# Sketched attention and a two-layer MLP on one core: token order 4gg+g, every x block turned by TensorE, shared PSUM banks, new orders

## The chip, the cores and the metric

The kernel runs on one core of one Trainium2 chip. The core has five engines that run side by side, each with its own queue of instructions in a fixed order: TensorE (PE, matrix products; PEld is its weight load), VectorE (DVE), ScalarE (ACT), GpSimd (POOL) and SyncE (SP, which here only issues transfers). Sixteen DMA engines move data between the chip's memory (DRAM) and the on-chip SBUF. Matrix products land in PSUM, which has eight banks of 128 partitions by 512 fp32 values.

The metric is the device time of one execution in microseconds (us), lower is better. A profile is one such execution recorded by the hardware; its span runs from the first to the last instruction.

## The reference

Attention with a polynomial sketch, then a layer norm with an MLP on the concatenated heads. B = 4 batches, H = 4 heads, S = 1088 tokens, D = 32, r = 8; q, k and v are float32. S1, S2 and the two MLP weights come as float64.

```python
def phi(x):                                  # 64 features a token and head
    a = np.einsum('rd,bhsd->bhsr', S1, x)
    b = np.einsum('rd,bhsd->bhsr', S2, x)
    return np.einsum('bhsi,bhsj->bhsij', a, b).reshape(*x.shape[:-1], r * r)
q_p, k_p = phi(q), phi(k)
kv  = np.einsum('bhsf,bhsd->bhfd', k_p, v)
z   = np.sum(k_p, axis=2)
num = np.einsum('bhsf,bhfd->bhsd', q_p, kv)
den = np.einsum('bhsf,bhf->bhs', q_p, z)[..., None] + 1e-06
x   = (num / den).transpose(0, 2, 1, 3).reshape(B, S, 128)
xn  = (x - mean(x)) / sqrt(var(x) + 1e-06) * g_ln
out = x + np.maximum(xn @ w_ch1, 0.0) @ w_ch2    # 128 -> 512 -> 128
```

## The kernel before

**Tiles.** The 1088 tokens of a batch are 32 runs of 34: run gg has 32 tokens, numbered 8g+u (g = 0 to 3, u = 0 to 7), and two rest tokens. Token 8g+u of run gg sits on partition 32g+gg of tile u, so a batch is 8 tiles of 128 tokens and a ninth (u = 8) of 64 rest tokens. Behind the attention four tiles make a chunk: chunks 2b and 2b+1 belong to batch b (c = 0 to 7), chunks 8 and 9 hold the rest tokens of batches 0, 1 and of 2, 3.

**Loads.** `ld` and `ld_u` (L115, L125) bring q and k with head and run on the partitions; `ld_v` (L133) brings v of one head, with 4 outer steps (g) of 32 runs in DRAM; `ld_vr` (L141) brings the rest tokens of v; `ld_w` (L150, L152) the MLP weights, 512 KB each. All but the two `ld_s` (S1, S2 on ACT's queue) and `ld_g` (g_ln, on POOL's) go through SP's queue. The framework gives SP's transfers eight semaphores in turn, so that each waits until the eighth before it has landed.

**A batch, in steps.**

- `turn_g`, `turn_u`, `turn_r` (L404, L412, L421; DVE): transposes of 32 by 32 blocks put q and k, head by dimension on the partitions and token on the free axis, into qT and kT. There is one pair for even and one for odd batches.
- `k_feat` (L451; PE) and `k_tok` (L460; DVE): a and b of k, turned to tokens on the partitions (kf). Batch 0 goes another way (`k_dir`, `k_cp`, `k_prod0`). `k_prod` (L85; POOL): the 64 products a token and head (kp). `k_sum`, `k_zs`, `k_sc`, `k_sccp` (L475, L483, L489, L497): the denominator's row for q.
- `k_val` (L504; PE): kv in bank KV; `k_vcp` (ACT), `k_spr` (L519; PE), `k_rcp` (ACT): kv copied and transposed into kvr.
- `q_feat` (L572; PE), `q_tok` (L581; DVE, two halves), `q_ac`, `q_den`, `q_rec` (DVE: product, sum and reciprocal for the denominator, units 0 to 4 and 4 to 9), `q_a2` and `q_prod` (L85; POOL: tiles a and qp), `q_turn` (L619; DVE: qp transposed into qpT). Batch 0 has `q_dir`, `q_ac0`, `q_b0`, `q_prod0` on PE and DVE.
- `num` (L633; PE): the numerator into banks X and Y, `num_cp` and `num_r` (ACT): copied into xT (features on the partitions).

**A chunk, in steps.** `hid` (L734; PE, one 128x512 product for each of four groups of hidden units, into bank M, N or O) and `relu` (L742; ACT) read xT. `sec` (L750; PE, four products a tile into one bank) reads hT. `fin` (L763; DVE) is sec times 1/sigma plus x, into ob; `store` (L784) sends ob out by SP, again with 4 outer steps of 32 runs, and `store_r` (L793) the rest tokens of a batch, one by SP and one by ACT. The layer norm's gain and mean are folded into w1 (`c_cg`, `fold`), so only 1/sigma is left: `st_bn`, `st_ag` (DVE), `st_pow` (L723; POOL).

**Rows of x.** `st_bn` and `fin` need x with tokens on the partitions. For chunks 0, 1, 8 and 9, `row_pe` (L684) transposes xT on PE into bank KV and `row_cp` copies it with ACT. For chunks 2 to 7 it goes through DRAM: `row_turn` (L693; DVE, blocks of 32 into xh), `row_wr` (L697; one transfer by SP into xd), `row_rd` (L702; four transfers back into x, each with 4 outer steps of 32). Two buffers of hT and ob, four of xT and x are reused in turn; ob takes the chunks in the order 0, 1, 2, 3, 8, 4, 5, 6, 7, 9.

**What sets the order.** Each step is an `op`, and a string `PROGRAM` lists them; an engine's queue holds its steps in the order of that string. `fill n w` puts n products of ones, w columns wide, on PE; nothing reads them. The weights' steps `w_ex` to `w_add` turn float64 words into float32 (s: S1, S2; 1 and 2: the MLP weights).

```python
through_dram = set((2, 3, 4, 5, 6, 7, ))     # L671
order = [0, 1, 2, 3, 8, 4, 5, 6, 7, 9]       # ob and hT: even place buffer 0, odd place buffer 1
```

Of the kernel before, what the change touches and what calls it, by code (L numbers as in the profile page):

```python
# [25 lines left out]
def kernel(  # L26
# [374 lines left out]
    @op  # L401
    def turn_g(x, b, g0, g1):
        dst, src = turned[x]
        dve.transpose(  # L404
            _ap(dst[b % 2], 0, P, 32 * g0, [[32, g1 - g0], [P, 8], [1, 32]]),
            src[b][:, 256 * g0 : 256 * g1],
        )
# [383 lines left out]
    def store_r(eng, c, i):  # L791
        b = 2 * (c - 8) + i
        by[eng].dma_start(  # L793
            out=bass.AP(out.tensor, out.offset + (b * S + 32) * DM,
                        [[DM, 2], [G * DM, 32], [1, DM]]),
            in_=obs[turn_of(c)][64 * i : 64 * i + 64, 0:P],
# [18 lines left out]
    q_dir 0 4 N; w_e3 V 1 0 256; ld_vr S 1 0; w_add G 1 256 512; turn_r q 0; turn_u q 0 4 8;
    k_val 0; w_e3 V 1 256 512; q_cp A 0 4 N 16 24; q_ac0 0 4 N 0; w_add G 1 0 256; q_den 0 0 4;
    q_rec 0 0 4; ld_vr S 1 1; w_low A 2 0 512; q_dir 4 9 O; w_mul G 1 0 256; q_b0 0 4 N 0;
    k_vcp A 0; q_prod0 0 2 N 0; w_mul G 1 256 512; q_prod0 2 4 N 0; k_spr 0; q_cp A 4 9 O 16 24;
    q_turn 0 2; k_rcp A 0; fold N 0 256; ld S k 2 0 34; turn_g k 1 0 4; num 0 0 2;
    fold_cp A N 0 256; turn_r k 1; num_cp A 0 0 0 2; q_turn 2 4; num_cp A 0 1 0 2; hid M 0 0 0 2;  # L820
    q_ac0 4 9 O 4; q_den 0 4 9; ld S q 2 0 34; hid N 0 1 0 2; q_rec 0 4 9; relu A M 0 0 0 2;
    turn_r q 1; ld_v S 2 0; num 0 2 4; q_b0 4 9 O 4; relu A N 0 1 0 2; q_prod0 4 9 O 4;
    ld_v S 2 1; fold M 256 512; ld_v S 2 2; num_cp A 0 1 2 4; num_cp A 0 0 2 4; ld_v S 2 3;
    row_pe 0 K; fold_cp A M 256 512; q_turn 4 9; ld_vr S 2 0; row_cp A 0 K; hid N 0 2 0 2;
    ld_vr S 2 1; hid M 0 3 0 2; relu A N 0 2 0 2; w_bits V 2 0 512; relu A M 0 3 0 2; num 0 4 9;
    turn_g q 1 0 4; w_mant A 2 0 512; ld S k 3 0 34; w_add G 2 0 512; hid M 0 1 2 4; turn_r k 2;
    num_r A 0; turn_g k 2 0 4; num_cp A 0 0 4 8; num_cp A 0 1 4 8; k_feat 1; relu A M 0 1 2 4;
    w_ex V 2 0 512; row_pe 1 K; ld S q 3 0 34; k_tok 1; w_exf A 2 0 512; hid M 0 3 2 4;
    ld_v S 3 0; turn_r q 2; row_cp A 1 K; k_prod G 1 5 9; w_e2 V 2 0 512; hid N 0 0 2 4;
    ld_v S 3 1; relu A M 0 3 2 4; st_bn 1; k_sum 1; relu A N 0 0 2 4; ld_v S 3 2; hid M 1 1 0 4;  # L830
    k_zs 1; turn_g q 2 0 4; ld_v S 3 3; ld_vr S 3 0; k_prod G 1 0 5; k_sc 1; ld_vr S 3 1;
    hid N 0 2 2 4; relu A M 1 1 0 4; k_sccp V 1; st_bn 0; q_feat 1; relu A N 0 2 2 4; st_ag 0;
    hid N 1 0 0 4; w_e3 V 2 0 512; k_val 1; st_pow 0; turn_r k 3; relu A N 1 0 0 4; q_tok 1 0;
    turn_g k 3 0 4; w_mul G 2 0 512; hid N 1 2 0 4; k_vcp A 1; turn_r q 3; q_tok 1 1; sec O 0 3;
    relu A N 1 2 0 4; q_ac V 1 0 4; q_den 1 0 4; sec O 0 2; q_ac V 1 4 9; q_rec 1 0 4; st_ag 1;
    q_a2 G 1 0 4; turn_g q 3 0 4; sec O 0 1; q_prod G 1 0 4; sec O 0 0; q_den 1 4 9; q_rec 1 4 9;
    hid M 1 3 0 4; fin O 0 0; fin O 0 1; q_a2 G 1 4 9; fin O 0 3; fin O 0 2; k_feat 2; q_turn 0 4;
    q_prod G 1 4 9; relu A M 1 3 0 4; store S 0; sec O 1 0; k_tok 2; sec O 1 1; k_prod G 2 5 9;
    q_turn 4 9; k_spr 1; sec O 1 2; k_rcp A 1; k_sum 2; num 1 0 9; k_prod G 2 0 5; k_zs 2; k_sc 2;
    num_cp A 1 1 4 8; sec O 1 3; num_cp A 1 1 0 4; k_sccp V 2; num_cp A 1 0 0 4; st_pow 1;  # L840
    num_r A 1; num_cp A 1 0 4 8; row_turn 2; k_val 2; row_turn 3; row_wr S 2; fin O 1 0;
    row_wr S 3; fin O 1 3; q_feat 2; fin O 1 2; k_vcp A 2; fin O 1 1; store S 1; hid N 2 0 0 4;
    q_tok 2 0; q_tok 2 1; row_rd S 2 3; hid M 2 1 0 4; relu A N 2 0 0 4; row_rd S 2 0;
    q_ac V 2 0 4; row_rd S 2 2; hid N 2 2 0 4; q_den 2 0 4; relu A M 2 1 0 4; q_rec 2 0 4;
# [69 lines left out]
```

## Time and profile before

| what | us |
|---|---|
| median of 3 runs (139.23 to 141.09) | 140.34 |
| the profiled execution | 141.0 |
| its span | 139.2 |
| mean TensorE clock granted, share of full | 0.891 |

How the views are read. The table of engines gives busy time and its share of the span. In the row of 40 slices each digit is the busy share of 3.48 us in tenths; PEclk is the clock that TensorE was granted. In the list of waits a row names who waited for whom, the total in us, how often, and the longest. In a table of windows the columns are from:to, length, busy us (and instructions) of PE, PEld, DVE, ACT and POOL, the clock granted, the mean busy share of the 16 DMA engines and GB/s. In a timeline the columns are start, duration, engine, line, operation, output<-input with shapes, and how many instructions the row merges; in brackets the idle time ahead of it and who ended it. A PE product of fp32 shows as two records, so x10 is five products. The chain of waits follows the work that ended last backwards. The lines themselves stand in the prediction.

### The profile page before, as it was taken

What the parts mean: (1) busy time and instruction counts of PE and PEld (TensorE: products, weight loads), DVE (VectorE), ACT (ScalarE), POOL (GpSimd) and SP (SyncE); (2) the same over time, 40 slices, a digit from 0 to 9 for tenths busy, and PEclk for the clock granted to TensorE, in tenths of its full rate; (3) what the DMA queues carried; (4) which work ended last, traced back from release to release, by engine and by line L of the source; (5) the groups of instructions that cost most, each with busy time, mean ns of one, the idle gap of its engine ahead of it and who ended that gap; (6) DMA issues with size and microseconds to landing.
All of it is one profiled execution on the core that took longest, in us unless ns stands there. A gap on an engine that the chain in (4) does not pass through costs nothing.

```text
span 139.2 us, 3266 instructions
## 1 busy us (share of the span) xinstructions
PE 105.5 (76%) x1336; PEld 72.0 (52%) x1336; DVE 75.8 (54%) x225; ACT 39.6 (28%) x99; POOL 49.4 (36%) x62
## 2 busy tenths in 40 slices
PE   5998598999986899999105999907999999970000
...
PEclk9999855699999999999975799996899999999555
...
GB/s 137 238 132 227 315 111 245 158 101 235 177 99 68 16 64 151 57 79 77 24 0 56 19 153 66 78 87 26 0 0 37 196 30 66 82 49 0 36 102 31
DMA packets 14023, 13.32 MB, mean 96 GB/s; under 512 B 1848, under 2 KB 11832, under 8 KB 14008
## 3 DMA queue, kind: packets, MB, share of 16 engines
...
q8 instruction: 10, 0.16, 0.5%
q10 hardware_dynamic: 164, 0.07, 0.2%
q14 instruction: 5, 0.04, 0.1%
q0 software_dynamic: 32, 0.00, 0.0%
...
## 4 chain that ended last, share of the span: by engine, by line
DMA 46%; SPq 16%; DVE 14%; PE 10%; POOL 4%; issue 3%; ACT 3%; DVEq 0%; ACTq 0%
DMA vn<-in_v_dram 15%; DMA x<-xd 12%; DMA xd<-xh 9%; SPq L702 9%; DMA kn<-in_k_dram 5%; DMA out_dram<-ob 4%; PE X L633 4%; SPq L133 3%; POOL qp L85 3%; DVE st L710 3%; PE M L734 3%; DVE qpT L619 3%; PE PO L750 3%; ACT xT L80 2%; DVE xh L693 2%
## 5 line engine op out<-in xcount | busy, mean ns | idle before, releaser
L734 PE MATMUL M<-xT,w 128*128 128x512 f32 (+1 forms) x72 | 34.8, 604 | 5.0 <-ACT hT L742 4.6
L742 ACT ACTIVATE hT<-M 128x512 f32<-128x512 f32 (+2 forms) x44 | 21.4, 500 | 36.5 <-PE M L734 30.1
L750 PEld LDWEIGHTS PO<-w,hT 128*128 128x128 f32 x208 | 25.1, 194 | 7.0 <-DVE ob L763 3.2
L750 PE MATMUL PO<-w,hT 128*128 128x128 f32 x208 | 26.4, 279 | 1.9 <-DVE ob L763 1.4
L723 POOL TENSOR_TENSOR rstd<-va,mhalf 128x4 f32<-128x4 f32 (+1 forms) x10 | 9.6, 957 | 48.7 <-DVE va L717 48.5
L710 DVE BATCH_NORM_STATS2 st<-x 128x6 f32<-128x128 f32 x32 | 7.0, 280 | 27.1 <-DMA x<-xd 27.0
L734 PEld LDWEIGHTS M<-xT,w 128*128 128x128 f32 x72 | 12.3, 201 | 15.2 <-ACT hT L742 10.3
L85 POOL TENSOR_TENSOR kp<-kf 128x1024 f32<-128x1024 f32 (+3 forms) x8 | 15.2, 1916 | 3.6 <-ACT kf L80 2.2
L85 POOL TENSOR_TENSOR qp<-a,fq 128x1024 f32<-128x1024 f32 (+1 forms) x6 | 13.0, 2171 | 0.4
L619 DVE STREAM_TRANSPOSE qpT<-qp 128x1280 f32<-128x1280 f32 (+2 forms) x9 | 11.1, 1228 | 2.5 <-POOL qp L85 2.4
L80 ACT COPY xT<-X 128x256 f32<-128x256 f32 (+1 forms) x18 | 5.4, 361 | 17.3 <-PE X L633 17.3
L633 PE MATMUL X<-qpT,kvr 32*32 32x288 f32 (+2 forms) x384 | 9.4, 404 | 0.3 <-DVE qpT L619 0.3
L750 PEld LDWEIGHTS X<-w,hT 128*128 128x128 f32 x64 | 7.8, 192 | 1.4 <-issue 1.4
L237 PE MATMUL M<-ones 128*128 128x256 f32 (+2 forms) x16 | 7.2, 574 | 1.5 <-DVE ones L181 1.5
L750 PE MATMUL X<-w,hT 128*128 128x128 f32 x64 | 8.0, 275 | 0.0
L475 PE MATMUL KV<-kf 128*32 128x32 f32 x72 | 1.7, 212 | 8.0 <-DVE kf L460 8.0
L763 DVE SCALAR_TENSOR_TENSOR ob<-PO,rstd,x 128x128 f32<-128x128 f32 x24 | 6.7, 337 | 1.8 <-PE PO L750 1.8
L633 PEld LDWEIGHTS X<-qpT,kvr 32*32 32x32 f32 x384 | 5.2, 119 | 3.6 <-issue 2.1
L305 POOL TENSOR_TENSOR mant<-mant,low 128x256 f32<-128x256 f32 (+1 forms) x3 | 2.9, 988 | 11.5 <-ACT mant L283 11.5
L581 DVE STREAM_TRANSPOSE fq<-X 128x576 f32<-128x576 f32 x6 | 4.4, 754 | 4.1 <-PE X L572 4.1
L504 PE MATMUL KV<-kp,vn 128*32 128x64 f32 x288 | 5.1, 221 | 1.2 <-DMA vn<-in_v_dram 1.1
L475 PEld LDWEIGHTS KV<-kf 128*32 128x32 f32 x72 | 1.2, 121 | 9.1 <-DVE kf L460 8.2
(115 smaller groups left out, 123.7 us busy)
## 6 DMA issues: line engine op xcount, KB each, us to landing
...
```

The source lines that it names most:

```text
L80: act.copy(o, i)
L85: by[eng].tensor_tensor(out=o, in0=a, in1=b, op=ALU.mult)
L237: pe.matmul(M[0][:, 0:w], ones[:, 0:P], ones[:, 0:w], start=True, stop=True)
L619: dve.transpose(_ap(qpT, 0, P, 32 * u0, [[32, u1 - u0], [TW, 8], [1, 32]]), qp[:, H * F * u0 : H * F * u1])
L633: pe.matmul(XS[r // 2][D * h : D * h + D, o : o + w], kvr[b % 2][rows, DM * f + D * h : DM * f + D * h + D], qpT[rows, c : c + w], start=( ...
L702: by[eng].dma_start(out=rows_of(c)[:, P * h : P * (h + 1)], in_=bass.AP(xd[c].tensor, xd[c].offset + 32 * P * h, [[P * P, 4], [P, 32], [1, ...
L710: dve.bn_stats(out=sts[slot(c)][:, 6 * t : 6 * t + 6], in_=row_ap(c, t))
L723: pool.tensor_tensor(out=rstds[slot(c)][:, 0:n], in0=vas[slot(c)][:, 0:n], in1=mhalf[:, 0:n], op=ALU.pow)
L734: pe.matmul(banks[z][:, 0:n], w1[:, P * j : P * (j + 1)], cols(c)[:, a : a + n], start=True, stop=True)
L742: act.activation(o, i, AF.Relu)
L750: pe.matmul(banks[z][:, DM * t : DM * (t + 1)], h[:, 512 * j + P * t : 512 * j + P * (t + 1)], w2[:, DM * j : DM * (j + 1)], start=(j == 0 ...
L763: dve.scalar_tensor_tensor(out=o, in0=i0, scalar=rstds[slot(c)][:, t : t + 1], in1=row_ap(c, t), op0=ALU.mult, op1=ALU.add)
```

## The change

1. **Token order.** Token 8g+u of a run sits on partition 4gg+g. `ld_v` and `store` now have 32 outer runs in DRAM with 4 steps inside; `turn_g` and `turn_u` write with a stride of 4 elements inside blocks, where before 32 elements lay side by side. Sizes are the same.
2. **Rows of x.** `through_dram` is empty: all ten chunks use `row_pe` and `row_cp`. The six `row_turn`, six `row_wr` and 24 `row_rd` are gone; six `row_pe` (four 128x128 transposes each) and six 128x512 `row_cp` on ACT are new.
3. **Shared banks.** `row_pe`, `sec` and `hid` now take M, N and O in turn; before, `sec` had O (at the end X and Y) and `row_pe` had KV. `fill` takes a bank as argument and mostly uses O.
4. **Rest tokens.** `store_r` sends 32 rows at a time, so there are eight instead of four, all by SP.
5. **New orders** of `PROGRAM`, on all queues; one `fill` more of 128x512 at the start, two new places with fills in batch 0's `num`, `c_act`, `c_vpad 2` and `c_vpad 3` late, `ld_v S 3 0` behind `store S 0`.

```diff
@@ ld_v
-                        [[8 * D, 4], [G * D, 32], [1, 8 * D]]),
+                        [[G * D, 32], [8 * D, 4], [1, 8 * D]]),
@@ fill
-    def fill(n, w):
+    def fill(n, w, z):
-            pe.matmul(M[0][:, 0:w], ones[:, 0:P], ones[:, 0:w], start=True, stop=True)
+            pe.matmul(banks[z][:, 0:w], ones[:, 0:P], ones[:, 0:w], start=True, stop=True)
@@ turn_g
-            _ap(dst[b % 2], 0, P, 32 * g0, [[32, g1 - g0], [P, 8], [1, 32]]),
+            _ap(dst[b % 2], 0, P, g0, [[1, g1 - g0], [P, 8], [4, 32]]),
@@ turn_u
-            _ap(dst[b % 2], 0, P, P * u0, [[32, 4], [P, u1 - u0], [1, 32]]),
+            _ap(dst[b % 2], 0, P, P * u0, [[1, 4], [P, u1 - u0], [4, 32]]),
@@
-    through_dram = set((2, 3, 4, 5, 6, 7, ))
+    through_dram = set(())
@@ store
-                        [[8 * DM, 4], [G * DM, 32], [1, 512]]),
+                        [[G * DM, 32], [8 * DM, 4], [1, 512]]),
@@ store_r
-        b = 2 * (c - 8) + i
+        b, j = 2 * (c - 8) + i // 2, i % 2
-            out=bass.AP(out.tensor, out.offset + (b * S + 32) * DM,
-                        [[DM, 2], [G * DM, 32], [1, DM]]),
-            in_=obs[turn_of(c)][64 * i : 64 * i + 64, 0:P],
+            out=bass.AP(out.tensor, out.offset + (b * S + 32 + j) * DM, [[G * DM, 32], [1, DM]]),
+            in_=obs[turn_of(c)][32 * i : 32 * i + 32, 0:P],
@@ PROGRAM (two lines of some 70)
-    ld_s A 0; ld_g; ld S k 0 0 16; c_small; c_ones; ld_s A 1; ld S k 0 16 34; c_iota;
...
+    ld S k 0 0 16; c_ones; ld_s A 0; c_vpad 1; ld S k 0 16 34; c_pads 1; ld_s A 1; c_pads 0;
...
```

What the new order does to the queues, at three places. First, DVE at the start: the conversion of S1 and S2 (ex, exf, bits, mant, s_f) and `c_cg` (cg from g_raw, which `ld_g` loads). Before:

```order
L264 TENSOR_SCALAR ex_115<-s_raw 8x64
L277 TENSOR_SCALAR exf_116<-ex_115 8x64
L295 TENSOR_SCALAR ex_115<-exf_116 8x64
L269 TENSOR_SCALAR bits_114<-s_raw 8x64
L404 STREAM_TRANSPOSE kT_102<-kn_73 128x2x8x32
L309 SCALAR_TENSOR_TENSOR mant_117<-s_raw,mant_117 8x64
L300 SCALAR_TENSOR_TENSOR bits_114<-s_raw,ex_115 8x64
L85 TENSOR_TENSOR s_f<-mant_117,bits_114 8x256
```

And of the change, the same place on DVE:

```order
L269 TENSOR_SCALAR bits_114<-s_raw 8x64
L337 TENSOR_SCALAR cg<-ident,g_raw 128x128
L277 TENSOR_SCALAR exf_116<-ex_115 8x64
L295 TENSOR_SCALAR ex_115<-exf_116 8x64
L300 SCALAR_TENSOR_TENSOR bits_114<-s_raw,ex_115 8x64
L309 SCALAR_TENSOR_TENSOR mant_117<-s_raw,mant_117 8x64
L85 TENSOR_TENSOR s_f<-mant_117,bits_114 8x256
```

`c_cg` moved from behind the first transposes of k and q to the middle of the conversion, and `ld_g`, which it waits for, moved on POOL's queue behind ten memsets and iotas.

Second, PE behind the last batch's numerator (X, Y <- qpT, the L633 rows). PO is bank O, M_67 and M_68 are M and N, xT_153 to xT_156 the four buffers of xT, xTr the rest tokens, ident the identity that transposes. Before:

```order
L633 MATMUL X_66<-qpT,kvr_143 32x288 x8
L750 MATMUL PO<-w_131,hT_187 128x128 x12
L684 MATMUL KV<-ident,xTr_158 128x128
L750 MATMUL PO<-w_131,hT_187 128x128 x4
L734 MATMUL M_68<-xT_155,w_130 128x512
L734 MATMUL M_67<-xT_155,w_130 128x512
```

And of the change:

```order
L633 MATMUL X_66<-qpT,kvr_143 32x288 x8
L750 MATMUL PO<-w_131,hT_188 128x128 x8
L684 MATMUL M_67<-ident,xT_154 128x128 x4
L684 MATMUL M_68<-ident,xT_155 128x128 x4
L750 MATMUL PO<-w_131,hT_188 128x128 x4
L684 MATMUL M_67<-ident,xTr_158 128x128
L750 MATMUL PO<-w_131,hT_188 128x128 x4
L684 MATMUL M_67<-ident,xT_156 128x128 x4
L734 MATMUL M_68<-xT_155,w_130 128x512
```

The transposes of three chunks moved here, among the second layer of chunk 4 (it was chunk 5 before: one chunk's second layer more is left behind the last numerator).

Third, SP's queue from the transfers of chunks 6 and 7 to the end (xd is the DRAM copy of x, ob the results). Before:

```order
L697 DMA xd_173<-xh_165 128x4x128
L697 DMA xd_174<-xh_166 128x4x128
L702 DMA x_161<-xd_173 128x1x128
L784 DMA out_dram<-ob_189 4x32x512
L702 DMA x_161<-xd_173 128x1x128 x2
L702 DMA x_162<-xd_174 128x1x128 x2
L702 DMA x_161<-xd_173 128x1x128
L702 DMA x_162<-xd_174 128x1x128 x2
L784 DMA out_dram<-ob_190 4x32x512
L784 DMA out_dram<-ob_189 4x32x512
L793 DMA out_dram<-ob_190 2x32x128
```

And of the change, from the stores of chunks 3 and 4 (one row) on:

```order
L784 DMA out_dram<-ob_190 32x4x512 x2
L793 DMA out_dram<-ob_189 32x128 x4
L784 DMA out_dram<-ob_189 32x4x512
L784 DMA out_dram<-ob_190 32x4x512
L793 DMA out_dram<-ob_190 32x128 x2
L784 DMA out_dram<-ob_189 32x4x512
L793 DMA out_dram<-ob_190 32x128 x2
```

The ten transfers of x are gone, four `store_r` of chunk 8 moved between the stores of chunks 4 and 5, and two of chunk 9's four stand behind the last store.

More of the change, by code (lines that the diff above doesn't have):

```diff
@@ L815 @@
[L815 to L844, printed above, removed]
@@ L845 @@
-    row_rd S 3 3; q_ac V 2 4 9; q_a2 G 2 0 4; row_rd S 2 1; hid M 2 3 0 4; q_den 2 4 9;
-    relu A N 2 2 0 4; row_rd S 3 2; q_prod G 2 0 4; q_rec 2 4 9; row_rd S 3 1; hid N 3 0 0 4;
-    relu A M 2 3 0 4; row_rd S 3 0; sec O 2 0; st_bn 2; relu A N 3 0 0 4; q_a2 G 2 4 9; st_ag 2;
-    sec O 2 3; q_turn 0 4; st_pow 2; sec O 2 1; st_bn 3; q_prod G 2 4 9; sec O 2 2; st_ag 3;
-    k_spr 2; hid M 3 1 0 4; fin O 2 3; k_rcp A 2; fin O 2 2; fin O 2 0; fin O 2 1; st_pow 3;
-    row_pe 8 K; q_turn 4 9; store S 2; k_feat 3; row_cp A 8 K; relu A M 3 1 0 4; hid N 3 2 0 4;
@@ L875 @@
[L875 to L878 removed]
+    ld S k 0 0 16; c_ones; ld_s A 0; c_vpad 1; ld S k 0 16 34; c_pads 1; ld_s A 1; c_pads 0;
+    ld_u S q 0 0 4; c_iota; ld_w S 1; c_ac 1; c_vpad 0; c_ac 0; ld_v S 0 0; ld_g; c_rest;
@@ new lines @@
+    k_val 1; k_tok 2; q_prod G 1 0 4; q_turn 4 9; row_pe 1 M; k_vcp A 1; k_spr 1; hid N 1 1 0 4;
+    k_rcp A 1; w_add G 2 0 512; relu A O 0 2 0 2; q_turn 0 4; k_sum 2; w_e3 V 2 0 512; num 1 0 9;
+    k_zs 2; st_bn 0; w_mul G 2 0 512; k_sc 2; num_cp A 1 1 0 4; st_ag 0; sec O 0 3;
+    relu A N 1 1 0 4; k_prod G 2 0 5; row_cp A 1 M; sec O 0 2; num_cp A 1 0 4 8; st_bn 1;
+    num_cp A 1 0 0 4; num_r A 1; sec O 0 0; turn_g q 2 0 4; hid N 2 1 0 4; sk_qq 2; st_pow 0;
+    sec O 0 1; c_vpad 2; st_ag 1; k_prod G 2 5 9; turn_r q 2; hid M 2 3 0 4; turn_r k 3;
```

107 lines of the change are left out of this document (67 added, 40 removed).

## The prediction

> **What bounds the kernel now.** I read the page first: the table of engines, the 40 slices, the shares of the chain that ended last.
>
> ```profile
> span 139.2 us, 3266 instructions
> PE 105.5 (76%) x1336; PEld 72.0 (52%) x1336; DVE 75.8 (54%) x225; ACT 39.6 (28%) x99; POOL 49.4 (36%) x62
> ...
> PE   5998598999986899999105999907999999970000
> ...
> PEclk9999855699999999999975799996899999999555
> ...
> DMA 46%; SPq 16%; DVE 14%; PE 10%; POOL 4%; issue 3%; ACT 3%; DVEq 0%; ACTq 0%
> ```
>
> PE is the busiest engine, but it stands nearly still three times: about slices 20, 27 and the last four. Transfers and their issue are 62% of the chain. Next I read the list of waits, and in the chain the place of the longest one.
>
> ```profile
> DVE st L710 <- DMA x<-xd: 27.0, 4, 14.5
> ...
> ACT hT L742 <- DVE st L710: 6.2, 1, 6.2
> ...
> DVE ob L763 <- DMA out_dram<-ob: 5.0, 1, 5.0
> ```
>
> ```profile
> 106.12 4.82 DMA xd<-xh
> ...
> 120.24 5.30 DMA x<-xd
> ```
>
> Four times `st_bn` waits for x on its way through DRAM, 27.0 us in all; DVE's queue behind it, `q_turn` and `fin` too, stands still. The 6.2 us on ACT are `store_r`, which ACT's own queue issued and which waited for a `fin` behind such an `st_bn`; `relu` stood behind it, and PE behind `relu`. The last wait is for a store. Then the windows, for the transfers' speed:
>
> ```profile
> 20.00:25.00 5.00, 4.61 (x134) 2.87 (x132) 4.86 (x10) 1.57 (x5) 0.00 (x0) 0.50 0.85 228
> ...
> 60.00:65.00 5.00, 5.00 (x45) 3.50 (x45) 0.00 (x0) 1.14 (x3) 0.00 (x0) 1.00 0.30 81
> ...
> 130.00:134.00 4.00, 0.00 (x0) 0.00 (x0) 0.00 (x0) 0.00 (x0) 0.00 (x0) 0.50 0.24 71
> ...
> 33.00:36.00 3.00, 2.86 (x39) 1.07 (x38) 2.97 (x12) 0.98 (x2) 3.00 (x2) 1.00 1.06 307
> ```
>
> From 130 to 134 only stores with four outer runs are under way, from 60 to 65 only such reads: a share of 0.24 and 0.30, 71 and 81 GB/s, so four or five of sixteen engines. With k and q among the loads (33 to 36) all are busy, 307 GB/s. [...]
>
> **The change, stage by stage.** Stage A, the start up to batch 0's first `num` (20.5 us before):
>
> ```profile
> 1.24 0.74 POOL L110 DMA_DIRECT2D g_raw<-in_moe_g_ln_dram  x1 [0.79 <-POOLq L898]
> ...
> 2.39 0.47 POOL L222 MEMSET vn<- 64x128 f32 x2
> ```
>
> ```profile
> 4.00 0.18 DVE L264 TENSOR_SCALAR ex<-s_raw 8x64 uint32<-8x64 uint32 x1 [0.54 <-DMA s_raw<-in_S_dram]
> ...
> 4.76 0.69 DVE L404 STREAM_TRANSPOSE kT<-kn 128x512 f32<-128x512 f32 x1
> ...
> 5.73 0.41 DVE L85 TENSOR_TENSOR s_f<-mant,bits 8x256 f32<-8x256 f32 x1
> ...
> 15.64 0.24 DVE L421 STREAM_TRANSPOSE qT<-qn 128x64 f32<-128x64 f32 x1 [2.50 <-DMA qn<-in_q_dram]
> ```
>
> ```profile
> g_raw<-in_moe_g_ln_dram POOLq DMA_DIRECT2D x1, 0.5 KB, 4.7
> ```
>
> The quick loads of v remove DVE's 2.5 us of waiting for q behind them. But `ld_g` is issued behind ten short memsets and iotas (0.1 to 0.2 us each, about 1.3), so g_raw lands at 1.24 + 1.3 + 4.7 = 7.2, and `c_cg`, which waits for it, now stands on DVE inside the conversion of S1 and S2. That took 4.00 to 6.14, 0.7 of it a transpose; nearly all of the other 1.4 is now behind g_raw, with `c_cg` itself some 0.2, so s_f ends near 8.7 instead of 6.1. That takes 2.6 back on the same DVE queue. I take 0; bounds -2.5 (the conversion is hidden) and +2.6 (q is late anyway). `c_act` and the two late `c_vpad` (0.2 each) lie in idle time of ACT and POOL; without that cover they cost 0.6. The longer fill at the start runs while PE waits for s_f.
>
> Stage B, to `num` of batch 1 (49.4 before). It hangs on DVE, then POOL:
>
> ```profile
> 16.70 0.28 DVE L85 TENSOR_TENSOR ac<-M,fq 128x128 f32<-128x128 f32 x1
> ...
> 24.53 1.51 DVE L619 STREAM_TRANSPOSE qpT<-qp 128x1280 f32<-128x1280 f32 x1
> 25.97 0.38 DVE L269 TENSOR_SCALAR bits<-w_raw 128x512 uint32<-128x512 uint32 x1
> ...
> 30.66 0.78 DVE L460 STREAM_TRANSPOSE kf<-X 128x576 f32<-128x576 f32 x1
> ...
> 40.61 0.74 DVE L581 STREAM_TRANSPOSE fq<-X 128x576 f32<-128x576 f32 x1
> ```
>
> ```profile
> 42.49 0.40 POOL L85 TENSOR_TENSOR a<-fq,rden 128x128 f32<-128x128 f32 x1 [3.70 <-DVE rden L601]
> ...
> 45.42 2.40 POOL L85 TENSOR_TENSOR qp<-a,fq 128x1280 f32<-128x1280 f32 x1
> ```
>
> ```profile
> L404 DVE STREAM_TRANSPOSE kT<-kn 128x1024 f32<-128x1024 f32 x3 | 3.6, 1201 | 0.0
> ```
>
> ```profile
> 49.42 1.60 PE L633 MATMUL X<-qpT,kvr 32*32 32x288 f32 x64 [0.34 <-DVE qpT L619]
> ```
>
> From 16.70 to 26.04 DVE does batch 0's q and one turn of k for batch 1; the change puts that turn (1.2) behind it: 24.8. Then four passes over weights (0.38 each, 1.5), the turn, `k_tok` 0.78: 28.3. Two turns (2.4) and two small ones (0.3), then two `q_tok` (1.5): 32.5, against 41.35 before. What stood between and is now behind: the statistics of chunks 0 and 1, two turns (q of batch 2, k of batch 3) and a step for the weights; k of batch 2 has landed by then if sixteen engines load at the 307 GB/s above. From the end of `q_tok` to POOL's `q_a2` 1.2, as before (41.35 to 42.49); both halves on POOL 42.49 to 47.82 = 5.3; the last `q_turn`, now the shorter one, 1.2. `num` at 32.5 + 7.7 = 40.2. PE has 14 us of work in the last 14.5 of that (first `num` parts, `hid` of chunks 0 and 1, features), so it is hardly ahead, and before, the clock was 0.50 up to 27 (the window of 20 to 25). I take 41.0; bounds 40.2 and 43.3 (5 us of that work at half clock).
>
> Stage C, from there on PE alone, if nothing holds it. Its work, priced by dense rows at full clock:
>
> ```profile
> 108.12 4.65 PE L734 MATMUL M<-xT,w 128*128 128x512 f32 x10
> ...
> 115.31 0.45 PE L734 MATMUL M<-xTr,w 128*128 128x128 f32 x2
> 115.59 1.02 PE L734 MATMUL M<-xT,w 128*128 128x512 f32 x2
> ...
> 118.55 3.74 PE L750 MATMUL X<-w,hT 128*128 128x128 f32 x32
> ```
>
> ```profile
> 30.41 0.66 PE L684 MATMUL KV<-ident,xT 128*128 128x128 f32 x4
> ...
> 52.26 1.21 PE L504 MATMUL KV<-kp,vn 128*32 128x64 f32 x72
> 53.40 0.79 PE L572 MATMUL X<-qT,skq 32*32 32x288 f32 x32
> ```
>
> - `hid`: six chunks of four, 24 x 0.93 = 22.3; rest tokens 8 x 0.28 (start to start) = 2.2.
> - `sec`: 34 tiles x 0.935 = 31.8.
> - `num`: 3 x 1.60 = 4.8.
> - `row_pe`: 6 x 0.66 + 0.5 = 4.5; this is the new work, 4.0 of it.
> - `k_val` 2 x 1.21, `q_feat` 2 x 0.79, and the small products of batches 2 and 3 (`k_feat`, `k_sum`, `k_sc`, `k_spr`, 0.3 to 0.7 each, seven) 2.7: together 6.7.
>
> Sum 72.3, so the last product ends at 113.3. The six new `row_cp` (some 0.6 each) lie in ACT's idle time, ACT being busy 28%; without that they would hold the `relu` behind them, 3.6. Where `hid` takes a bank that `fin` still reads, PE waits for DVE: by the same rows three such places have DVE late by 0.3 to 0.5 (`fin` of chunks 1, 2 and 5, the last behind the four `store_r` of chunk 8, which SP issues ahead of store 5): +1.2. The gone `row_turn` freed 4 us of DVE that nothing waits for then. So 114.5.
>
> Stage D, the tail:
>
> ```profile
> 102.91 1.13 DVE L763 SCALAR_TENSOR_TENSOR ob<-PO,rstd,x 128x128 f32<-128x128 f32 x4 [1.84 <-PE PO L750]
> ```
>
> ```profile
> 128.08 1.84 SPq L784 DMA_DIRECT2D out_dram<-ob  x2
> ...
> 134.70 0.53 SPq L793 DMA_DIRECT2D out_dram<-ob  x1
> ```
>
> Before, the last `fin` waited for a store that shared four engines with another; with sixteen that wait is over before the `fin` is due. Left are four `fin` 1.1, three issues on SP (store 7, two `store_r`: 0.6 + 1.1 + gaps = 1.8), and from the last issue's end to the span's end, as before, 139.2 - 135.2 = 4.0: 6.9. The span: 121.4. The profiled execution took 141.0 with a span of 139.2, so +1.8: 123.2; it stood 0.7 over the median, so the forecast is **122.5 us**. Of the 17.8 gained, B gives 8.4, the tail 7.8 (14.7 from the last product to the end before), C 1.6, although it holds more work.
>
> **The rivals.**
>
> - *The clock falls once more in stage C.* For it: from 20 to 25 the grant was 0.50 with PE busy 4.61 of 5, so busy alone does not keep it. Against: from 28 to 66 all slices stand at 9. A stretch as long as the one around 17 to 27 (10.2 us) costs 5.1: 127.6.
> - *The strided turns are slower.* No row shows a DVE write with a stride of 4; the same operation with dense runs of 32 takes 1201 ns for 1024 elements, which is nearest, so I take no cost. A gain is excluded, the elements being as many; as the upper end each element takes twice as long. Ahead of batch 1's `num` stand four turns like the one of 0.69 in A and three of 1.2: +6.4, so 128.9. [...]
> - *32 outer runs spread no wider.* Then the 2.5 at q stay (+2.6 with the late s_f), and the last `fin` waits 3 for store 6: 128.1. Against: k and q, with many runs outside, fill all engines.
> - *Slower: the shared banks tie PE to DVE.* At seven places in stage C PE waits for a `fin` before the next `hid`, and DVE's queue can hold that `fin` behind a `q_turn` that waits for POOL (2.40 and 1.95 a half). At 3 us each it is +21, 143.5, and from there it decides. Against: the rows put DVE late by 0.5 at most.
>
> **How the numbers follow.** Chances: forecast 0.67, clock 0.16, strided turns 0.07, no wider spread 0.06, banks 0.04. The forecast's own range is 118.3 to 126 (the bounds of A and B, no waits at banks). The range of 117.5 to 129.5 takes in the next three cases and leaves out the last, and about a tenth beside it. Over and under 2% is about what three runs each can tell apart. Faster 0.95: all cases but the last, which I split into 0.03 slower and 0.02 within 2% (shorter waits).
>
> **What would show it.** Right: no wait of `st_bn` for a DMA; `num` of batch 1 near 41, of batch 3 near 85 (17 `sec`, eight long `hid`, three `row_pe` and itself, 28 us, are left); PE at 9 from there to the tail; DMA share well over 0.3 while a store is alone; the last four `fin` some 7 us before the end. Wrong: PE idle ahead of the M, N or PO products with DVE `ob` as releaser (banks); PEclk at 5 between slices 12 and 32 (clock); L404 rows over 1.3 us (strides); s_f before 7 us, or q still awaited (A).

## The result, and the profile after

| what | before | after |
|---|---|---|
| median, us | 140.72 (139.23 to 142.81, 4 runs) | 122.65 (122.26 to 124.07, 4 runs) |
| span of the profiled execution, us | 139.2 | 120.1 |

The ratio is 0.877 (95% interval 0.865 to 0.888): 18.1 us less, 0.15 us from the forecast. The stages behind that sum did not come out as forecast, and that is what the rest is about. The last step, from the span to the median, did not either: forecast were 121.4 and 1.1 on top, measured are 120.1 and 2.55.

The page of the changed kernel, the lines that answer to those of before:

```profile
span 120.1 us, 3282 instructions
...
PE 107.5 (90%) x1366; PEld 77.3 (64%) x1366; DVE 74.3 (62%) x219; ACT 42.4 (35%) x105; POOL 48.3 (40%) x62
...
PE   5909999989979994999999999999999999999930
...
PEclk9985555579999999999999999999999999999995
...
DMA  3988999870000000000004200002200001120202
...
PE 59%; DVE 20%; POOL 9%; DMA 5%; issue 2%; ACT 2%; DVEq 0%; POOLq 0%
```

PE's row has nines from slice 17 to the tail where before there were three holes. Transfers and their issue, 62% of the chain before, are about 5%. Loads end in the ninth slice (before 27 us). But the clock's row has fives from slice 4 to 8, where before it had two at the start (slices 6 and 7).

The stages as windows, cut at the first `num` of batch 0, the `num` of batch 1 and the end of the last product. The columns again: from:to, length, busy us of PE, PEld, DVE, ACT and POOL, clock, DMA share, GB/s. After:

```profile
0.00:26.01 26.01, 21.10 (x154) 16.72 (x154) 15.94 (x51) 6.93 (x19) 7.30 (x28) 0.67 0.88 286
26.01:46.63 20.62, 18.33 (x409) 10.74 (x409) 17.14 (x26) 9.43 (x25) 11.37 (x8) 1.00 0.04 12
46.63:115.13 68.50, 68.10 (x804) 49.80 (x804) 40.12 (x140) 26.06 (x62) 29.61 (x26) 1.00 0.09 31
115.13:120.10 4.97, 0.00 (x0) 0.00 (x0) 1.13 (x4) 0.00 (x0) 0.00 (x0) 0.74 0.19 66
```

Before, the same four:

```profile
0.00:20.52 20.52, 16.99 (x154) 11.79 (x154) 15.32 (x46) 7.21 (x19) 8.90 (x32) 0.90 0.66 195
20.52:49.42 28.90, 26.03 (x460) 17.68 (x459) 24.83 (x60) 10.64 (x27) 15.22 (x10) 0.89 0.48 136
49.42:124.50 75.08, 62.48 (x724) 42.58 (x724) 31.04 (x97) 21.80 (x53) 23.30 (x19) 0.93 0.24 64
124.50:139.20 14.70, 0.02 (x1) 0.00 (x0) 4.62 (x25) 0.00 (x0) 2.01 (x2) 0.66 0.14 41
```

| stage | before | forecast | after | after less forecast |
|---|---|---|---|---|
| A, to the first `num` | 20.5 | 20.5 | 26.0 | +5.5 |
| B, to `num` of batch 1 | 28.9 | 20.5 | 20.6 | +0.1 |
| C, to the last product | 75.1 | 73.5 | 68.5 | -5.0 |
| D, the tail | 14.7 | 6.9 | 5.0 | -1.9 |
| span | 139.2 | 121.4 | 120.1 | -1.3 |

Two errors of five microseconds with opposite signs made the forecast of the span good, and that forecast, still 1.3 too long, met a step from the span to the median that was taken 1.5 too short. That the total was hit to 0.15 us is luck. In the list of waits of the changed kernel the 27.0 us of `st_bn` for a transfer are gone, and no `fin` waits for a store:

```profile
DVE st L710 <- ACT x L80: 1.9, 2, 1.1
DVE cg L337 <- DMA g_raw<-in_moe_g_ln_dram: 1.5, 1, 1.5
...
PEld M L734 <- DVE ob L763: 1.1, 2, 0.7
PEld M L750 <- DVE ob L763: 1.0, 1, 1.0
```

The start on DVE's timeline (start, duration, engine, line, operation):

```profile
4.03 1.07 DVE L404 STREAM_TRANSPOSE kT<-kn 128x512 f32<-128x512 f32 x1
...
7.55 0.28 DVE L337 TENSOR_SCALAR cg<-ident,g_raw 128x128 f32<-128x128 f32 x1 [1.51 <-DMA g_raw<-in_moe_g_ln_dram]
...
8.64 0.41 DVE L85 TENSOR_TENSOR s_f<-mant,bits 8x256 f32<-8x256 f32 x1
```

The product of PE that waited for s_f (sk below), the numerator's start, and two pairs from the middle of stage C:

```profile
9.20 0.99 PE L357 MATMUL KV<-ident,s_f 8*128 8x8 f32 x4 [3.00 <-DVE s_f L85]
...
26.01 0.86 PE L633 MATMUL X<-qpT,kvr 32*32 32x64 f32 x64 [0.46 <-ACT kvr L80]
...
105.39 1.02 PE L734 MATMUL PO<-xT,w 128*128 128x512 f32 x2
106.25 1.95 PE L750 MATMUL M<-w,hT 128*128 128x128 f32 x16
...
113.17 1.06 PE L750 MATMUL M<-w,hT 128*128 128x128 f32 x8
114.06 1.06 PE L750 MATMUL PO<-w,hT 128*128 128x128 f32 x8
```

The groups of the strided turns and the transfers' landing times (KB each, median us):

```profile
L404 DVE STREAM_TRANSPOSE kT<-kn 128x1024 f32<-128x1024 f32 x3 | 6.4, 2122 | 0.0
L404 DVE STREAM_TRANSPOSE qT<-qn 128x1024 f32<-128x1024 f32 x3 | 6.3, 2091 | 0.0
```

```profile
out_dram<-ob SPq DMA_DIRECT2D x8, 256.0 KB, 2.4
...
out_dram<-ob SPq DMA_DIRECT2D x8, 16.0 KB, 1.5
```

A turn of 1024 elements takes 2.1 us in place of 1.20. A store lands in 2.4 us. While the store of chunk 1 is alone (67.0 to 67.5) the 16 engines' share is 0.87, at 336 GB/s; before, stores alone had 0.24 and 71 (130 to 134). So the 32 outer runs do spread a store over nearly all engines, as the prediction assumed.

### The profile page after: what moved, and what is told of

Same layout as the page of the kernel before. It is cut to its first block, busy times and chain, and to the rows that moved or that the text cites. A ratio compares the mean times of both kernels' runs of the same rounds, so it can differ in the third digit from the quotient of the medians.

```text
span 120.1 us, 3282 instructions
## 1 busy us (share of the span) xinstructions
PE 107.5 (90%) x1366; PEld 77.3 (64%) x1366; DVE 74.3 (62%) x219; ACT 42.4 (35%) x105; POOL 48.3 (40%) x62
## 4 chain that ended last, share of the span: by engine, by line
PE 59%; DVE 20%; POOL 9%; DMA 5%; issue 2%; ACT 2%; DVEq 0%; POOLq 0%
PE M L750 11%; PE M L734 10%; PE PO L750 9%; PE X L633 6%; POOL qp L85 5%; DMA g_raw<-in_moe_g_ln_dram 5%; DVE qT L404 5%; DVE fq L581 3%; PE PO L734 3%; DVE kT L404 3%; PE PO L237 2%; PE X L433 2%; PE M L684 2%; PE PO L539 2%; PE KV L504 2%
## 5 line engine op out<-in xcount | busy, mean ns | idle before, releaser
L734 PE MATMUL M<-xT,w 128*128 128x512 f32 (+1 forms) x58 | 25.6, 556 | 0.0
L85 POOL TENSOR_TENSOR kp<-kf 128x1024 f32<-128x1024 f32 (+3 forms) x8 | 15.1, 1892 | 12.2 <-ACT kf L80 11.7
L750 PEld LDWEIGHTS M<-w,hT 128*128 128x128 f32 x144 | 16.8, 192 | 2.7 <-ACT hT L742 1.1
L750 PE MATMUL M<-w,hT 128*128 128x128 f32 x144 | 17.8, 278 | 0.2 <-DVE ob L763 0.2
L750 PE MATMUL PO<-w,hT 128*128 128x128 f32 x128 | 16.3, 277 | 0.1
L750 PEld LDWEIGHTS PO<-w,hT 128*128 128x128 f32 x128 | 15.2, 192 | 1.6 <-issue 1.4
L85 POOL TENSOR_TENSOR qp<-a,fq 128x1280 f32<-128x1280 f32 (+1 forms) x6 | 13.0, 2173 | 0.2
L763 DVE SCALAR_TENSOR_TENSOR ob<-M,rstd,x 128x128 f32<-128x128 f32 x16 | 4.4, 338 | 9.4 <-PE M L750 5.3
L633 PE MATMUL X<-qpT,kvr 32*32 32x288 f32 (+2 forms) x384 | 7.7, 332 | 2.0 <-DVE qpT L619 1.5
L237 PE MATMUL PO<-ones 128*128 128x512 f32 (+2 forms) x16 | 7.6, 613 | 1.4 <-DVE ones L181 1.4
L404 DVE STREAM_TRANSPOSE kT<-kn 128x1024 f32<-128x1024 f32 (+1 forms) x5 | 8.5, 1698 | 0.0
L633 PEld LDWEIGHTS X<-qpT,kvr 32*32 32x32 f32 x384 | 4.5, 103 | 4.6 <-DVE qpT L619 2.4
L734 PE MATMUL PO<-xT,w 128*128 128x512 f32 (+1 forms) x14 | 6.8, 569 | 0.0
```

Source lines behind the costliest of these rows:

```text
L85: by[eng].tensor_tensor(out=o, in0=a, in1=b, op=ALU.mult)
L237: pe.matmul(banks[z][:, 0:w], ones[:, 0:P], ones[:, 0:w], start=True, stop=True)
L404: dve.transpose(_ap(dst[b % 2], 0, P, g0, [[1, g1 - g0], [P, 8], [4, 32]]), src[b][:, 256 * g0 : 256 * g1],)
L633: pe.matmul(XS[r // 2][D * h : D * h + D, o : o + w], kvr[b % 2][rows, DM * f + D * h : DM * f + D * h + D], qpT[rows, c : c + w], start=( ...
L734: pe.matmul(banks[z][:, 0:n], w1[:, P * j : P * (j + 1)], cols(c)[:, a : a + n], start=True, stop=True)
L750: pe.matmul(banks[z][:, DM * t : DM * (t + 1)], h[:, 512 * j + P * t : 512 * j + P * (t + 1)], w2[:, DM * j : DM * (j + 1)], start=(j == 0 ...
```

## The experiments

Four questions: what made stage A late, what the strided turns cost, what the spread of the transfers and the rows by PE are each worth, and whether stage C really is PE alone. Spans and marks are of one profiled execution; medians are of 4 to 6 runs. The kernel before had medians of 139.6 to 141.3 beside them.

**The changed kernel once more**, as the anchor.

> The changed kernel once more, as the anchor for the others on the same chip. Both theories: 122.6 us, first num of batch 0 near 26, num of batch 1 near 46.6, last product near 115.

121.44 (120.7 to 123.14), span 119.5. s_f done at 8.90, first `num` 24.79, `num` of batch 1 at 46.03, last product done 114.54. So the first `num` moves by more than 1 us from one execution to the next; stage C is again 68.5.

**`c_cg` out of the conversion.**

```diff
-    w_bits V 0 0 64; c_cg V; w_mant A 0 0 64; ...
+    w_bits V 0 0 64; w_mant A 0 0 64; ...
-    ... turn_r k 0; w_exf A 1 0 256;
+    ... turn_r k 0; c_cg V; w_exf A 1 0 256;
```

> The changed kernel with c_cg moved behind turn_r k 0 on DVE, so that the conversion of S1 and S2 no longer stands behind g_raw. Theory (the chain from s_f to num of batch 1 carries the time): s_f ends near 7.4 instead of 9.05, so 1.7 less; PE's idle time ahead of it shrinks from 3.0 to about 1.2, and if that idle time is what brought the half clock, k_dir also takes 2.4 instead of 4.1: num of batch 1 near 43.5 to 45, the time 119.4 to 121. Rival (the wait is hidden, PE or transfers bound the start): num of batch 1 and the time move by less than 0.7.

120.02 (119.11 to 121.02), 1.4 less than the anchor beside it, and `num` of batch 1 at 44.74, both inside the theory's ranges. Its stages, and two rows of PE's timeline:

```profile
0.00:22.40 22.40, 18.45 (x155) 13.63 (x155) 16.32 (x50) 6.85 (x19) 7.46 (x28) 0.85 0.86 272
22.40:44.74 22.34, 18.54 (x409) 10.79 (x409) 17.58 (x27) 9.40 (x25) 11.36 (x8) 1.00 0.22 71
44.74:113.22 68.48, 68.09 (x804) 49.79 (x804) 40.12 (x140) 26.08 (x62) 29.65 (x26) 1.00 0.09 31
```

```profile
7.40 0.61 PE L357 MATMUL KV<-ident,s_f 8*128 8x8 f32 x4
...
28.36 0.46 PE L633 MATMUL X<-qpT,kvr 32*32 32x160 f32 x5 [1.34 <-issue]
```

The wait for g_raw in that place cost 1.65 us at s_f (8.90 to 7.25) and 2.4 at the first `num`. 1.3 of it lasts to the end. B is 1.1 longer than in the anchor and holds a stop of PE of 1.34 inside the third part of `num`, for which the profile names no releaser.

**The turns dense again**, with loads and stores as changed.

```diff
@@ turn_g
-            _ap(dst[b % 2], 0, P, g0, [[1, g1 - g0], [P, 8], [4, 32]]),
+            _ap(dst[b % 2], 0, P, 32 * g0, [[32, g1 - g0], [P, 8], [1, 32]]),
@@ turn_u
-            _ap(dst[b % 2], 0, P, P * u0, [[1, 4], [P, u1 - u0], [4, 32]]),
+            _ap(dst[b % 2], 0, P, P * u0, [[32, 4], [P, u1 - u0], [1, 32]]),
```

> The changed kernel with turn_g and turn_u writing dense runs of 32 as before. The tokens of q and k then stand in another order than those of v and of the stored rows, so the values of the output are other ones; every instruction, size and transfer is kept. Theory (strided writes cost 0.37 a half turn and 0.9 a long one, and four and three of them stand on the chain ahead of num of batch 1): the L404 rows return to 1.2, num of batch 1 comes 4.2 earlier at 42.4, the time is 118.4. Rival (DVE is not what limits the start, PE at half clock is): the rows return to 1.2, but the time moves by less than 1.5.

120.2 (119.22 to 120.43), 1.2 less. The turns took 1.23 and 1.21 us again, but the first `num` came at 25.17 and that of batch 1 at 45.04, only 1.0 earlier, not 4.2: under the new order DVE has room for most of what the stride costs. The time moved as the rival had it (less than 1.5); its reason, PE at half clock, is taken up below.

**The stride moved from DVE's writes to PE's reads**: turns of batches 1 to 3 dense, `k_feat` and `q_feat` read with a stride of 32 elements.

```diff
-                ... _ap(kT[b % 2], 64 * hp, 64, 32 * g, [[P, NU], [1, 32]]),
+                ... _ap(kT[b % 2], 64 * hp, 64, 8 * g, [[P, NU], [1, 8], [32, 4]]),
```

> The changed kernel with dense turns for batches 1 to 3, where k_feat and q_feat read kT and qT with a stride of 32 in eight groups of four instead; the rest tokens and the zero pads are laid out to fit. Batch 0 keeps the strided turns. Theory (DVE pays for the stride, PE's moving operand does not): three long turns ahead of num of batch 1 are 0.9 shorter, so 2.7 less there, time 119.9, k_feat and q_feat rows unchanged at 0.71 and 0.77. Rival (PE pays as much as DVE did): these rows rise to 1.4, two of them ahead of num of batch 1, time 121.5 to 123.

122.25 (120.52 to 122.77): no gain, inside the rival's range. The turns took 1.2 us, but `k_feat` rose from 0.71 to 1.18 and `q_feat` from 0.77 to 1.23, so the stride was paid on PE instead.

**Token order and transfers as before, all else as changed** (the dense turns, and four outer runs for v and stores).

```diff
@@ ld_v
-                        [[G * D, 32], [8 * D, 4], [1, 8 * D]]),
+                        [[8 * D, 4], [G * D, 32], [1, 8 * D]]),
@@ store
-                        [[G * DM, 32], [8 * DM, 4], [1, 512]]),
+                        [[8 * DM, 4], [G * DM, 32], [1, 512]]),
```

> The old token order with the changed kernel's orders, rows of x by PE and shared banks: loads of v and stores have 4 outer runs again, the turns write dense runs again. Against the run with dense turns and 32 runs (120.2 us, span 118.2) only the transfers differ. Theory A (the spread of transfers is worth time at both ends): loads end some 10 us later (near 35 to 40 in place of 25), q or a v is awaited at the start, the store at the end takes 5 to 6 us to land in place of 2.4: 124 to 130 us. Rival (with the transfers of x gone, four engines are enough): within 1.5 us of 120.2.

130.36 (130.26 to 131.12), a little above theory A's range. Its waits and its last two stages:

```profile
DVE ob L763 <- DMA out_dram<-ob: 9.5, 3, 6.0
...
PE M L734 <- DVE ob L763: 2.5, 1, 2.5
```

```profile
44.51:116.98 72.47, 69.76 (x804) 50.64 (x804) 36.06 (x139) 26.08 (x62) 29.59 (x26) 0.98 0.11 27
116.98:128.50 11.52, 0.00 (x0) 0.00 (x0) 1.39 (x5) 0.00 (x0) 0.00 (x0) 0.72 0.18 45
```

Against the run with dense turns, where only the transfers differ, the span is 10.3 longer, all of it in C and D: `fin` waits three times for a store, once with PE behind it, and right behind that wait the clock is at half for 3.4 us (105.1 to 108.5; a product of a long `hid` takes 1.92 us there, 1.02 elsewhere). The start, which theory A also made later, is not later, although by the slices loads go on to about 40 us: `num` of batch 1 comes at 44.51 (45.04 there).

**Only the rows of x by PE, in the kernel before**: `through_dram` empty, `row_pe` and `row_cp` (banks M and N) where `row_turn` stood, no transfers of x.

```diff
-    through_dram = set((2, 3, 4, 5, 6, 7, ))
+    through_dram = set(())
-    ... row_turn 2; k_val 2; row_turn 3; row_wr S 2; ...
+    ... row_pe 2 M; row_cp A 2 M; k_val 2; row_pe 3 N; row_cp A 3 N; ...
...
```

> The kernel before, with only the rows of chunks 2 to 7 taken from PE (row_pe into M or N in place, copied by ACT) and the transfers of x gone; order, token order and banks otherwise as before. Theory A: the trip of x through DRAM cost PE about 10 us of standing still behind num of batch 1, of which 4 go into the new transposes, and the start and the tail (4-run stores) stay: 132 to 137 us. Rival B: the rows by PE are nearly the whole gain: below 128. Rival C: the orders and the spread are what counts, rows by PE alone bring nothing: above 139.

122.82 (121.81 to 123.38), below 128, as rival B had it. Since this run also put chunk 4's rows into a bank that was still to be read, it was repeated with another bank.

> The kernel before with the rows of chunks 2 to 7 taken from PE and nothing else changed, now with chunk 4's rows in bank N (in the run of 122.8 us they were put in M ahead of the relu that still had to read chunk 8's values there, which changed part of the rest tokens' results). Theory (the trip of x through DRAM held nearly the whole gain): 121.5 to 124, num of batch 1 near 49.7, the last product near 113, 8 to 9 us behind it. Rival (the quick time came from that bank mix-up): above 130.

123.83 (123.2 to 124.2), ratio 0.878 (0.870 to 0.886): as fast as the whole change within the intervals, and as the theory had it. My first range of 132 to 137 was far off. The first stages together, C and D:

```profile
0.00:48.53 48.53, 42.91 (x612) 30.54 (x612) 39.47 (x105) 18.40 (x46) 24.05 (x42) 0.89 0.54 164
48.53:112.73 64.20, 62.58 (x748) 43.92 (x748) 31.93 (x114) 24.95 (x59) 25.30 (x21) 1.00 0.11 27
112.73:121.70 8.97, 0.00 (x0) 0.00 (x0) 0.45 (x2) 0.00 (x0) 0.00 (x0) 0.63 0.18 55
```

C alone shrank from 75.1 to 64.2, although it holds the new transposes, and the tail from 14.7 to 9.0.

**The same with the new token order** (turns, `ld_v` and `store` as changed).

> The same, with the new token order too (32 outer runs for v and stores, turns with a stride of 4), in the old order of the program. Theory (the spread is worth 3 to 4 at the tail, where stores with 4 runs land 8.6 us behind the last product, and the turns' extra 0.9 us each is hidden behind PE): 117 to 119.5 us, 5 to 6 us behind the last product. Rival (DVE, with nine turns of 0.4 to 0.9 us more, sets the old order's middle): num of batch 1 at 52 or later, time 121.5 to 125.

124.17 (123.31 to 124.65), no gain:

```profile
0.00:51.85 51.85, 43.21 (x612) 30.45 (x612) 45.99 (x105) 18.23 (x46) 24.15 (x42) 0.90 0.49 156
51.85:116.05 64.20, 62.59 (x748) 43.93 (x748) 32.06 (x114) 24.95 (x59) 25.32 (x21) 1.00 0.07 27
116.05:121.90 5.85, 0.00 (x0) 0.00 (x0) 0.39 (x2) 0.00 (x0) 0.00 (x0) 0.77 0.18 56
```

The theory held for the tail alone (5.85); the total and the middle went as the rival had it (`num` of batch 1 at 51.85, just under its 52). DVE is busy 6.5 longer ahead of `num` of batch 1, which comes 3.3 later; C is the same to the hundredth; the tail is 3.1 shorter.

**Four more products in stage C.**

```diff
+    fill 1 512 O;      (ahead of hid of chunks 3, 4, 7 and of sec of chunk 4)
```

> The changed kernel with four more products of ones 128x512 (nothing reads them; 0.86 each at full clock) on PE in stage C, ahead of hid of chunks 3, 4, 7 and of sec of chunk 4. Theory (PE alone bounds stage C): all of it is seen, +3.0 to +3.6 on the changed kernel's 121.4 to 122.7, so 124.5 to 126.2. Rival (waits for DVE at the shared banks have slack that takes it): +0 to +1.5.

124.86 (124.05 to 125.43), inside the range. One window tells more than the total, since the start of this execution was late by itself (first `num` 26.42):

```profile
47.01:118.31 71.30, 71.11 (x812) 51.50 (x812) 39.87 (x140) 26.07 (x62) 29.62 (x26) 1.00 0.09 30
```

C grew by 2.8 of the 3.4 us put in (71.30 against 68.50). So C is bound by PE. The other 0.6 went into slack: the two waits of PE that the anchor shows there, 0.18 for `q_tok` (fq) and 0.17 for `fin`, are gone, and the rest was not placed.

**PE kept busy until s_f comes.**

```diff
-    fill 3 512 O; fill 1 128 O; sk;
+    fill 5 512 O; fill 1 384 O; fill 1 128 O; sk;
```

> The changed kernel with 2.4 us more of filling products before s_f arrives, so that PE does not stand idle from 6.7 to 9.0. Theory (that idle time let the clock fall at 9, and the clock is what made the way to the first num longer): the clock stays full till the next gap near 14, first num at 22 to 23.8 in place of 24.8 to 26.0, time 119.5 to 121. Rival (the clock falls then whatever PE does, or DVE sets the first num): first num 24.5 to 26, time within 0.5 of 121.4 to 122.7.

121.8 (121.27 to 122.91): no gain. The clock did stay at 1.00 until 17.3, and then fell to 0.50 for 6.8 us. It fell once more, for 3.4 us in stage C (48.0 to 51.4, slice 17), with PE busy throughout:

```profile
PEclk9999985599999999599999999999999999999997
...
9.60:17.30 7.70, 5.78 (x57) 4.88 (x57) 6.70 (x17) 3.60 (x11) 3.03 (x4) 1.00 0.98 320
17.30:24.10 6.80, 6.80 (x92) 5.90 (x91) 5.43 (x16) 1.19 (x4) 1.41 (x2) 0.50 0.87 295
```

PE used most of its full clock to wait: 1.4 us for DVE's zT (`k_zs`), which it had not waited for in the anchor. From sk to the first `num` it took 15.1 us, 0.6 less than in the anchor, but sk came 0.5 later (9.56, 0.3 of it behind the fills), so the first `num` came at 24.69 (24.79 in the anchor), as the rival had it. With the second fall C took 69.88 (45.83 to 115.71) in place of 68.50.

**`c_cg` moved, and the later gaps filled too** (1.9 us more of fills ahead of `k_sum` and `k_sc`).

> The run with c_cg behind turn_r (120.0 us, clock 0.50 from 14.3 to 21.1, first num 22.4), with 1.9 us more of filling products where PE stood idle at 11.3 and from 12.6 to 14.0. Theory (the clock falls after these gaps, and PE sets the first num there): the clock stays at 1.00 to beyond 20, first num at 20.0 to 21.5, time 118.5 to 119.7. Rival (DVE and POOL set the first num): 22 to 23, time 119.7 to 121.

121.21 (118.11 to 121.44): the runs lie too far apart to rank it. The clock fell to 0.50 all the same, from 10.2 to 17.0, and the first `num` came at 22.76, in the rival's range, so the theory failed.

**`c_cg` moved, the masks ahead of the conversion, the last two `store_r` on ACT's queue.**

```diff
-    w_ex V 0 0 64; ld_v S 0 1; turn_g k 0 0 2; c_ident; ld_v S 0 2; c_small; c_masks; ld_v S 0 3;
+    c_small; c_masks; w_ex V 0 0 64; ld_v S 0 1; turn_g k 0 0 2; c_ident; ld_v S 0 2; ld_v S 0 3;
-    ... store S 7; store_r S 9 3; store_r S 9 0;
+    ... store S 7; store_r A 9 3; store_r A 9 0;
```

> The kernel with c_cg behind turn_r (120.0 us, span 118.1, s_f done at 7.25, first num 22.4, 5.95 from the start of the last product to the end), with two more moves: the masks (c_small, c_masks, 0.9 us on DVE) ahead of the first conversion step, into DVE's wait for S1 and S2, and the last two store_r on ACT's queue, so that SP issues nothing behind the last store. Theory A (DVE's conversion sets the start): s_f done at 6.2 to 6.6, first num 21.0 to 21.9, half of it kept at num of batch 1 (44.0 to 44.5). Theory B (the issue of two store_r behind the last store is 1.0 us of the tail): 4.9 to 5.3 from the start of the last product to the end. Both: 118.2 to 119.4 us. Rival: the clock's fall lands elsewhere and takes the start's gain, and the landing of the store alone fixes the end: 119.7 to 121.

118.73 (117.28 to 119.54), ratio 0.850 (0.839 to 0.860): the interval lies below the changed kernel's 0.877 (0.865 to 0.888), and this is the fastest of all.

```profile
0.00:22.39 22.39, 19.42 (x154) 14.10 (x154) 16.33 (x50) 6.88 (x19) 7.44 (x28) 0.77 0.88 278
22.39:43.32 20.93, 18.57 (x408) 10.84 (x408) 17.71 (x27) 9.42 (x25) 11.36 (x8) 1.00 0.21 69
43.32:111.82 68.50, 68.10 (x804) 49.81 (x804) 40.12 (x140) 26.07 (x62) 29.65 (x26) 1.00 0.09 31
111.82:116.40 4.58, 0.00 (x0) 0.00 (x0) 1.13 (x4) 0.00 (x0) 0.00 (x0) 1.00 0.20 72
```

The total was met, the parts were not. s_f was done at 6.36 as expected, but PE was still at its fills until 7.28, and the first `num` stayed at 22.39. Against the run with `c_cg` moved, B lacks the stop of 1.34, and the tail gave 0.3, not 0.7 to 1.0.

## Why the total was right and the stages were not

The change in three parts: the rows of x by PE; the token order, with its transfers and turns; the new order of the program, with the shared banks and the split `store_r`. In profiled spans, one execution each, all with the rows of x by PE (before, with x through DRAM: 139.2):

| | old token order | new token order |
|---|---|---|
| old order of the program | 121.7 | 121.9 |
| new order | 128.5 | 119.5 |

**What the gain is made of.** Taking x's rows from PE is 17.5 of the 19.7 by itself. The 2.2 left are not shown to be a gain: spans of the anchor alone run from 118.6 to 121.1, and the ratios to the kernel before are 0.878 with the rows alone, 0.880 (0.872 to 0.889) with the token order too and 0.877 for the whole change. Only 128.5 stands apart (0.940, 0.933 to 0.947). So the new order needs the new token order, and not the other way round. The new token order costs DVE 0.9 a turn ahead of `num` and gives the tail three back, which cancels under the old order. The new order has DVE room for the turns, but its last stores stand closer, and with four outer runs `fin` waits 9.5 us for them. The prediction gave B 8.4, the tail 7.8 and C 1.6 of the gain; measured are 2.8 (A and B together), 9.7 and 6.6. It put the whole tail down to the spread, but 5.7 of it went with x's trip through DRAM alone (14.7 to 9.0); and it priced the new C without asking what the trip cost the old one, where PE was busy 62.5 of 75.1 us, at a mean clock of 0.93.

**A failed**: 26.0 where "I take 0" left 20.5; "+2.6" was there as a bound and was the right end, and even that was short by 2.9. The step to s_f was nearly right (8.7 forecast, 9.05 measured; 6.14 before). Wrong was the credit of 2.5 for q: it leaves 11.8 us from the end of s_f to the first `num`, and there were 17.0 (14.4 before). q is no longer awaited, as forecast, but the wait was DVE's, and the stretch was full of PE's work. Before, PE was busy for 12.35 of the 14.23 us from sk to the first `num`, so the end of another engine's wait could give at most 1.9. In the old order the stretch took 14.71 us (6.25 to 20.96), with DVE waiting 1.1 for q, and with the new token order, where DVE does not wait but is busy 1.1 longer, 14.76 (7.01 to 21.77); PE was busy for 14.2 in both. It took 15.0 with `c_cg` moved, 15.7 in the anchor and 16.8 in the profiled execution (PE busy for 16.35, at a mean clock of 0.52). So the first `num` follows sk by some 15 us, and the lateness of s_f went through whole: it is 2.9 of the 5.5, and the longer stretch is 2.6. Moving `c_cg` shows its share: 1.65 less at s_f, 2.4 less at `num`. Neither sign named for an error in A (s_f before 7 us, q still awaited) came.

**The clock** was taken as it was before, and there the prediction had no term. It was 0.50 for 17.1 us in the profiled execution, 13.7 in the anchor and 6.8 with `c_cg` moved, against 10.2 before, of which 3.9 lay ahead of the first `num` (16.6 to 20.5):

```profile
8.35:25.40 17.05, 16.20 (x146) 14.64 (x146) 12.25 (x35) 4.69 (x15) 4.32 (x6) 0.50 0.96 318
```

With 17.1 the stretch after sk is 1.1 longer than with 13.7, and that 0.7 longer than with 6.8, so up to 1.8 of A's error goes with the clock; no run changes the clock alone. What makes it fall is not settled. In most of these runs it falls within 1.3 us of the end of an idle time of PE, but filling one idle time moved the fall to the next (first `num` unchanged), and with both filled it fell while PE was busy. The four lengths are near 2, 3, 4 and 5 times 3.41 us, which is what the shortest fall in the kernel before lasted (95.10 to 98.51, at 0.50). Nor is it settled what brings the full clock back: here PE was busy in 16.2 of 17.05 us, without a gap from 9.20 on, and the clock stayed at 0.50 to the end of that stretch. So in this run a busy PE did not bring it back at once.

**B was right by length** (20.5 forecast, 20.6 measured), partly by luck: the last `q_tok` ended 13.0 after the first `num` in place of 12.0, and the 0.8 put in for PE was not needed; from there to `num` it took 7.66 (7.7 forecast). The strided turns took 1.75 times as long (the half ones 1.55): 0.9 us more a long turn, 0.4 a half one. But the wait that ends last in B is not DVE's queue alone: dense turns shorten the time from the first `num` to that of batch 1 by 1.4 (21.24 in the anchor, 19.87), and the total by 1.2. The step "put that turn behind it: 24.8 ... 32.5" holds as an order of work; its times started from A's, which had moved. The factor of 2 at the rival's end was the author's estimate and no run shows it; 1.75 and 1.55 are what the runs showed in its place. Why the stride costs DVE time was not shown.

**C was mis-sized**: 73.5 forecast, 68.5 measured, as a bound by PE right (68.10 of 68.50 busy, 2.8 of 3.4 us of added work seen). The term that failed is the price from durations of rows. A row of one long `hid` lasts 1.02 us and the next starts 0.86 after it; a tile of `sec` lasts 1.06 and the next starts 0.89 after it. Priced by such starts, 24 `hid` are 20.6 (forecast 22.3), 34 `sec` 30.3 (31.8), six `row_pe` and the small ones 3.1 (4.5), the rest tokens 1.8 (2.2), three `num` 4.6 (4.8), the others 5.7 (6.7): 66.1 in place of 72.3. The remaining 2.4, against 1.2 forecast for waits, are 0.4 in which PE is idle and rows that start later than in the densest places, which was not taken apart further.

**D was mis-sized** by 1.9: `fin` and SP's issues took 2.9 as forecast, but from the last issue to the end 2.1, not 4.0. Two parts of the change are behind that. With the new stores but the old `store_r` (two outer runs, in the old order) the last issue ends at 117.35 and the span at 121.9, 4.55 later; with the new `store_r` but stores of four outer runs it is 122.63 and 128.5, 5.9 later. Only both together gave 2.1: a 256 KB store lands in 2.4 us now, a `store_r` of 16 KB in 1.5. That transfers of 32 outer runs get sixteen engines, as A's loads of v and the sum for D took it, was the author's estimate, which no row of before shows for this shape; what the changed kernel showed is their mean share of 0.87 at 336 GB/s for a store alone (67.0 to 67.5), and 0.88 at 286 in stage A, with k and q among the loads.

**The rivals.** The clock fell, but in A, where no rival put it; in C of the changed kernel it was 1.00. In the run with PE kept busy until s_f it did fall in C once, for 3.4 us, which cost 1.4 and not 5.1. No wider spread: wrong, 10.3 us of span lie on it under the new order. Strided turns: right in the row, 1.2 us in the time. Banks: 0.2 us of PE's own waiting for `fin`.
